# Fourier mixing and a gated feed-forward network: batch 0's row E in column tiles, by way of DRAM, with another order of the first stage

## The chip, the cores and the metric

The kernel runs on one core of a Trainium2 chip. The engines of a core are TensorE (PE: matmuls into PSUM; PEld is its weight load), VectorE (DVE), ScalarE (ACT), GpSimd (POOL) and SyncE (SP, which only issues transfers here; ScalarE and GpSimd issue some as well). Each engine carries out its own queue in order and waits on semaphores. The metric is the device time of one execution in microseconds; the kernel before takes 1946.41 us, the median of three runs (1944.94 to 1950.29).

## The reference

```python
def _attn_ref(x):                      # x: (8, 3008, 256)
    X = np.fft.fft(x, axis=1)
    X = np.fft.fft(X, axis=2)
    return X.real.astype(np.float32)

def _moe_ref(x, w_gate, w_val, w_out): # x: that result as (24064, 256); d_ff = 1536
    gate = 1.0 / (1.0 + np.exp(-(x @ w_gate)))
    val = x @ w_val
    return (gate * val @ w_out).astype(np.float32)
```

The weights come as float64 and are turned into float32 on the chip.

## The kernel before, in words

**The algebra.** The transform along the 256 features is multiplied into the weights: `merge` (L316) multiplies a piece of a weight by the table `dt` and puts the halves into `G1` (cosine rows 0 to 127) and `G2` (row 0 is the cosine row 128, the rest are sine rows). What is left for each batch is the transform along the 3008 tokens: `pk` (128 folded features with cosines), `qk` (127 with sines) and one more row, E (feature 128, with cosines). By symmetry only 1505 tokens are computed; token S-k follows from the same two sums with one sign turned.

**Sequence stage.** A batch is folded fourfold (`fold_ops`) and split into two blocks, for even and odd frequencies. The six slices `q` of a block are multiplied by a table (`ST`, cosines and sines, 377 or 376 columns) and summed into two PSUM banks `ev` and `od` (`half`); `places` adds and subtracts these into `pk` and `qk`. For batch 0 this stands in front of everything. Its E row is a third cosine group (`what` = 2): the E column is broadcast to 128 columns of the stationary matrix, so that all 128 partitions get the same row (`ek`, the third tile of `PQE[0]`). It is stored to the DRAM row `ed[0]` for later chunks. Batches 1 to 7 get their E rows together (`e_sums`): the stationary matrix has 7 columns, four column tiles of 32 hold the two blocks and the two parities of `q`, and the rows go to DRAM and come back as a broadcast (`e_rows`, tile `ek`).

**Gate groups.** A batch has six chunks of 252 (the last 246) tokens, a chunk has twelve groups `i`, one for each 128 of the 1536 hidden features. A group: `seed` takes a PSUM bank `pf` and ScalarE writes E times `ge` (row 0 of `G2`, turned onto the partitions by small transfers in `merge`) into its two halves; `front_a` adds the `pk` products; `part` copies the value (`ae`) for the mirrored tokens; `front_b` adds the `qk` products; `gate_a` and `gate_b`, one turn later, do sigmoid and product for both token halves on ScalarE and VectorE; `back` multiplies by the output weights into the banks `po`. In the very first chunk (groups 0 to 11) `seed` writes nothing. Groups 0 to 4 (`N1` = 5) add E with a matmul of `G2` by `e0`, a tile that is zero but for row 0; groups 5 to 11 have E in row 0 of `qk` and take it out again on VectorE (L614, L632).

**Weights.** A weight piece `j` (`jobs[j]`: gate, value or output, and which 256 columns or rows) is loaded by SyncE (`weight_load`), taken apart by two passes on ScalarE (`weight_parts`), joined by three operations on VectorE and an addition on GpSimd (`weight_join`), and then merged (`weight_use`: four matmuls, two ScalarE copies into `G2` and `G1`, two small `ge` transfers). Pieces 0 to 9 are loaded at the start, the others from when batch 0's input is no longer needed.

**Order.** The order on each engine is that of the program text. First come the loads, pieces 0 and 1, the folds and sequence sums with `weight_round` between the evacuations, and merge 2; then the loop over `i`. In turn `i`: `front_a(i)`, `gate_a(i-1)`, `part(i)`, `seed(i+1)`, `gate_b(i-1)`, then what `pre` and `use` hold (joins, parts and merges of later pieces), `back`, `front_b(i)`, and what `side` holds. PSUM has eight banks: five for products (`po0` to `po4`), three that `pf`, merges and sums take by turns.

## Time and profile before

| | |
|---|---|
| median of 3 runs | 1946.41 us (1944.94 to 1950.29) |
| profiled execution | 1944.18 us, span 1942.4 us |
| TensorE clock, mean granted | 0.996 |
| TensorE busy | 1913.1 us, 98% |
| first sequence matmul of batch 0 | 21.72 us |
| first gate group | 48.3 us |
| 36 sequence matmuls of batch 0 | 21.72 to 46.6 us |

Busy time is the union of an engine's instructions. A matmul in float32 appears as two passes, so that x4 are two matmuls; the ends of matmuls are modelled. A row of the timeline has the start in us, the duration in us, engine, line, operation, tiles written and read, shapes, the number of instructions merged into the row and, in brackets, the idle time before it with what ended it. SPq and ACTq are transfers that an engine issues. The chain is followed back from the last instruction to whatever released each step. In the table of waits a row says who waited for whom, with the sum in us, the number of times and the longest.

### The profile page before, as it was taken

The numbers are of one execution on the slowest core, as the hardware profiler recorded it, in microseconds if no ns is written. First come the engines' busy times: TensorE is split into PE (matmuls) and PEld (weight loads), VectorE is DVE, ScalarE is ACT, GpSimd is POOL, SyncE is SP. The second block draws the span as 40 slices with busy tenths as digits, with TensorE's granted clock in tenths as the row PEclk, the third lists the DMA queues.
The fourth block names the chain that finished last, engine by engine and source line by source line (L and its number), as shares of the span: only waits on it lengthen the run. The fifth ranks groups of instructions, "written<-read, shape, count | busy, mean of one in ns | idle before, by whom it ended". The sixth has DMA issues, their size and how long they took to land.

```text
span 1942.4 us, 34340 instructions
## 1 busy us (share of the span) xinstructions
PE 1913.1 (98%) x11180; PEld 1778.8 (92%) x11180; DVE 1445.2 (74%) x3250; ACT 1332.0 (69%) x3120; POOL 1565.7 (81%) x2802
## 2 busy tenths in 40 slices
PE   6999999999999999999999999999999999999997
PEld 4789989999999999999999999999999999999997
DVE  7667887787777877777777776777777777777776
ACT  3577657766777677776777767777677766777775
POOL 4269989997889788987889879888788986777776
PEclk9999999999999999999999999999999999999999
DMA  8343422212022111212112121111200100011011
GB/s 273 106 127 37 109 72 54 55 20 79 15 53 54 54 39 20 76 25 79 20 41 60 16 83 23 47 46 25 82 14 14 25 17 14 14 25 17 14 20 27
DMA packets 171978, 96.78 MB, mean 50 GB/s; under 512 B 136090, under 2 KB 163868, under 8 KB 169252
## 3 DMA queue, kind: packets, MB, share of 16 engines
q1 hardware_dynamic: 169842, 94.06, 20.3%
q8 instruction: 90, 1.47, 0.3%
q10 hardware_dynamic: 1926, 0.52, 0.1%
q14 instruction: 88, 0.72, 0.1%
q0 software_dynamic: 32, 0.00, 0.0%
HBM read 69.83 MB, written 46.71 MB: 60 GB/s over the span
## 4 chain that ended last, share of the span: by engine, by line
PE 96%; DVE 3%; DMA 1%; ACT 1%; issue 0%; SPq 0%; DVEq 0%
PE pf L134 49%; PE po L134 41%; PE ev L134 3%; PE od L134 1%; DVE c L719 1%; PE ps L134 1%; DMA x<-in_xf_dram 1%; DVE z L635 0%; ACT pf L648 0%; DVE h L649 0%; DVE h L647 0%; DVE os L729 0%; PE pe L134 0%; DVE x L428 0%; DVE x L392 0%
## 5 line engine op out<-in xcount | busy, mean ns | idle before, releaser
L655 POOL TENSOR_TENSOR sf<-h 128x168 f32<-128x168 f32 (+1 forms) x940 | 521.4, 574 | 225.6 <-DVE h L649 225.6
L655 POOL TENSOR_TENSOR sf<-h,sf 128x168 f32<-128x168 f32 (+1 forms) x1128 | 629.2, 578 | 59.1 <-DVE h L649 58.7
L134 PE MATMUL pf<-qk,G 128*128 128x252 f32 (+1 forms) x2304 | 582.7, 376 | 2.0 <-ACT ae L611 2.0
L134 PE MATMUL pf<-pk,G 128*128 128x252 f32 (+1 forms) x2304 | 582.8, 376 | 0.0
L649 DVE TENSOR_TENSOR h<-pf,z 128x252 f32<-128x252 f32 (+1 forms) x576 | 241.6, 419 | 427.7 <-ACT pf L648 427.7
L595 ACT ACTIVATE pf<-ek,ge 128x252 f32<-128x252 f32 (+1 forms) x1128 | 531.6, 471 | 18.5
L134 PE MATMUL po<-sf,wf 128*128 128x168 f32 (+1 forms) x3008 | 518.7, 305 | 0.0
L611 ACT ACTIVATE ae<-pf 128x504 f32<-128x504 f32 (+1 forms) x569 | 335.5, 590 | 234.9 <-PE pf L134 234.0
L134 PEld LDWEIGHTS pf<-pk,G 128*128 128x128 f32 x2304 | 436.4, 190 | 52.8 <-issue 1.6
L134 PEld LDWEIGHTS po<-sf,wf 128*128 128x128 f32 x3008 | 462.7, 190 | 8.1
L134 PE MATMUL po<-h,wf 128*128 128x168 f32 (+2 forms) x2640 | 469.2, 306 | 0.0
L719 DVE TENSOR_TENSOR c<-c 128x168 f32<-128x168 f32 (+1 forms) x929 | 438.5, 504 | 5.4 <-ACT c L696 0.2
L134 PEld LDWEIGHTS pf<-qk,G 128*128 128x128 f32 x2304 | 410.3, 190 | 34.8 <-ACT ae L611 3.3
L134 PEld LDWEIGHTS po<-h,wf 128*128 128x128 f32 x2640 | 420.1, 190 | 17.2 <-issue 0.9
L635 DVE TENSOR_TENSOR z<-ae,pf 128x504 f32<-128x504 f32 (+1 forms) x569 | 378.6, 665 | 25.2 <-ACT h L630 23.4
L630 ACT ACTIVATE h<-pf 128x252 f32<-128x252 f32 (+1 forms) x576 | 218.0, 379 | 161.3 <-PE pf L134 156.7
L648 ACT ACTIVATE pf<-z 128x252 f32<-128x252 f32 (+1 forms) x576 | 214.4, 372 | 105.7 <-DVE h L647 103.2
L647 DVE TENSOR_TENSOR h<-h,pf 128x252 f32<-128x252 f32 (+1 forms) x576 | 232.5, 404 | 0.0
L655 POOL TENSOR_TENSOR sf<-sf 128x168 f32<-128x168 f32 (+1 forms) x188 | 108.5, 577 | 14.7
L655 POOL TENSOR_TENSOR sf<-sf,h 128x168 f32<-128x168 f32 (+1 forms) x188 | 102.9, 547 | 0.0
L696 ACT COPY c<-po 128x504 f32<-128x504 f32 (+1 forms) x141 | 80.2, 569 | 2.6 <-PE po L134 2.6
L134 PE MATMUL ev<-st,x 63*128 63x189 f32 (+3 forms) x372 | 72.4, 345 | 7.7 <-DVE x L398 7.7
(141 smaller groups left out, 891.8 us busy)
## 6 DMA issues: line engine op xcount, KB each, us to landing
x<-xr SPq DMA_DIRECT2D x14, 1536.0 KB
out_dram<-os SPq DMA_DIRECT2D x372, 56.0 KB
xr<-in_xf_dram SPq DMA_DIRECT2D x14, 768.0 KB
xr<-in_xf_dram SPq DMA_DIRECT2D x35, 256.0 KB
ek<-ed SPq DMA_DIRECT2D x39, 126.0 KB
out_dram<-os SPq DMA_DIRECT2D x284, 7.0 KB
st<-in_stab_dram SPq DMA_DIRECT2D x4, 1111.9 KB
x<-in_xf_dram SPq DMA_DIRECT2D x2, 1512.0 KB
```

Of the source, the lines that this page charges most:

```text
L134: nc.tensor.matmul(o, l, r, start=start, stop=stop, skip_group_check=True)
L595: nc.scalar.activation(PF[i][:, g], EK[i // NFT], AF.Copy, scale=ge[:, g, f : f + 1])
L611: nc.scalar.activation(AP[i], PF[i], AF.Copy, scale=2.0)
L630: nc.scalar.activation(H[p][:, fh, 0:n], PF[i][:, 0], AF.Sigmoid)
L635: nc.vector.tensor_tensor(z[:, :, ::-1], AP.pop(i), PF[i], op=ALU.subtract)
L647: nc.vector.tensor_tensor(h[:, fh, 0:n], h[:, fh, 0:n], pf[:, 1], op=ALU.mult)
L648: nc.scalar.activation(pf[:, 0], z[:, 0], AF.Sigmoid)
L649: nc.vector.tensor_tensor(h[:, fh, n:], pf[:, 0], z[:, 1], op=ALU.mult)
L655: nc.gpsimd.tensor_tensor(block(p, dst), block(p, a), block(p, b), op=(ALU.subtract, ALU.add)[op])
L696: (nc.vector.tensor_copy if t == 1 or t == 3 and not last else nc.scalar.copy)(C[0][:, 3 * t * R : 3 * (t + 1) * R], PO[t][:, 0 : 3 * R])
L719: engine.tensor_tensor(t[:, dst * R : (dst + 1) * R], *v, op=(ALU.subtract, ALU.add)[op])
```

## The change

- Batch 0's E row is computed as those of the other batches: `e_sums(1)` with a stationary matrix of one column in four column tiles of bank `po4`, interleaved with the cosine groups. ScalarE copies and VectorE places it, ScalarE stores it to `ed[0:1]`, and `e_rows(0)`, issued on ScalarE as well, reads it back as a broadcast.
- `seed` writes E into PSUM for the first twelve groups too. `e0`, the extra `G2` matmuls, and the VectorE forms of `part` and `gate_a` go.
- Both sine tables are loaded ahead of piece 2.
- The second half of batch 0's fold runs wholly on VectorE; GpSimd's share of it goes.
- The order in front of the first group is new: block 0's cosines, E and block 1's by halves of `q`; then E's evacuation and store, half of the sines, piece 2 and its merge, the other sines with pieces 3 and 5 and their merges. Merges from piece 3 on go by turns into the product banks 4, 2 and 3. In the loop the pieces 6, 8, 9, ... follow with one turn between join and merge; `jobs` has its output pieces later.

```diff
     assert NPR == 6
-    jobs = [(0, 0), (1, 0), (0, 1), (1, 1), (2, 0), (0, 2), (1, 2), (2, 1), (0, 3), (1, 3), (0, 4), (2, 2),
-            (1, 4), (0, 5), (1, 5), (2, 3), (2, 4), (2, 5)]
+    jobs = [(0, 0), (1, 0), (0, 1), (1, 1), (2, 0), (0, 2), (1, 2), (2, 1), (0, 3), (1, 3), (0, 4), (1, 4),
+            (0, 5), (1, 5), (2, 2), (2, 3), (2, 4), (2, 5)]
     RAW, WS = {}, {}
     shared = {}
     KEEP = 10
...
     WO = {}
-    def weight_use(j, other=None):
+    turns = itertools.count()
+
+    def weight_use(j):
         w, c = jobs[j]
         if w == 2:
             WO[c] = WS.pop(j)
         else:
-            merge(WS.pop(j), w, c, other)
+            merge(WS.pop(j), w, c, (4, 2, 3)[next(turns) % 3] if j > 2 else None)
     def merge(ws, g, c, other):
         cs = slice(c * WC, (c + 1) * WC)
...
             ops += [lambda q=q: feat(pool, *parts[0], q) for q in qs]
         else:
-            def half1(q):
+            def half_rows(q):
                 point(nc.vector, 2, 3, q)
                 first(nc.vector, 2, 3, q)
                 for blk in range(2):
                     across(nc.vector, blk, q)
                     feat(nc.vector, *parts[blk], q)
-
-            def half2(q):
-                across(nc.vector, 0, q)
-                feat(nc.vector, *parts[0], q)
-                across(pool, 1, q)
-                feat(pool, *parts[1], q)
             for q in qs:
                 point(nc.vector, 0, 1, q)
             first(nc.vector, 0, 1, slice(0, NQ))
-            point(pool, 2, 3, qs[1])
-            first(pool, 2, 3, qs[1])
-            ops += [lambda: half1(qs[0]), lambda: half2(qs[1])]
+            ops += [lambda q=q: half_rows(q) for q in qs]
         for blk, (v, r) in enumerate(parts):
             if b and blk:
                 W[b, blk] = v[:, :, HD:D], r[:, :, HD:D]
                 continue
-            W[b, blk] = (v[:, :, 0:HD], r[:, :, 0:HD],
-                         v[:, :, HD : HD + 1].to_broadcast([v.shape[0], NQ, P]))
+            W[b, blk] = v[:, :, 0:HD], r[:, :, 0:HD], v[:, :, HD : HD + 1]
         return ops
...
     def seq_start(b):
         PQE[b] = [pqp.tile([P, NK + 1], F32, name=name, tag=name) for name in ("pk", "qk")]
-        if not b:
-            PQE[b].append(op.tile([P, NK + 1], F32, name="ek", tag="os"))
         for t in PQE[b]:
             nc.vector.memset(t[:, NK:], 0.0)
...
         tt(x8[:, :, 1], x8[:, :, 0], x8[:, :, 2], op=ALU.add)
         tt(x8[:, :, 3], x8[:, :, 0], x8[:, :, 2], op=ALU.subtract)
-    def e_sums():
+    def e_sums(m=B - 1):
         ps = bank("pe", NB - 1)
-        m = B - 1
         at_ = lambda blk, par: slice((2 * blk + par) * TB, (2 * blk + par) * TB + m)
-        for q in range(0, NQ, 2):
-            for blk in range(2):
-                c0, n = ((0, NE), (NE, NO))[blk]
-                for par in range(2):
-                    mm(ps[at_(blk, par), 0:n], x8[:, :, 1 + 2 * blk, q + par],
-                       ST[0][0:NP, 0, q + par, c0 : c0 + n], q == 0, q == NQ - 2)
-        er = op.tile([P, NK + 1], F32, name="er", tag="os")[0:m]
-        nc.vector.memset(er[:, NK:], 0.0)
-        a = evp.tile([P, 2 * NJ], F32, name="a", tag="a")[0:m, 0:NE]
-        e1 = evp.tile([P, 2 * NJ], F32, name="a", tag="a")[0:m, 0:NE]
-        nc.scalar.copy(a, ps[at_(0, 1), 0:NE])
-        nc.scalar.copy(e1[:, 0:NO], ps[at_(1, 0), 0:NO])
-
-        places(er, 0, True, a, ps[at_(0, 0), 0:NE])
-
-        def rest():
-            nc.scalar.copy(a[:, 0:NO], ps[at_(1, 1), 0:NO])
-
-        def last():
-            places(er, 1, False, e1[:, 0:NO], a[:, 0:NO])
-            nc.sync.dma_start(out=ed[1:], in_=er)
-        return rest, last
+
+        def sums(*qs):
+            for q in qs:
+                for blk in range(2):
+                    c0, n = ((0, NE), (NE, NO))[blk]
+                    w = x8[:, :, 1 + 2 * blk, q] if m > 1 else W[0, blk][2][:, q]
+                    mm(ps[at_(blk, q % 2), 0:n], w, ST[0][0:NP, 0, q, c0 : c0 + n], q < 2, q >= NQ - 2)
+
+        def even():
+            er = op.tile([P, NK + 1], F32, name="er", tag="os")[0:m]
+            nc.vector.memset(er[:, NK:], 0.0)
+            a = evp.tile([P, 2 * NJ], F32, name="a", tag="a")[0:m, 0:NE]
+            e1 = evp.tile([P, 2 * NJ], F32, name="a", tag="a")[0:m, 0:NE]
+            nc.scalar.copy(a, ps[at_(0, 1), 0:NE])
+            nc.scalar.copy(e1[:, 0:NO], ps[at_(1, 0), 0:NO])
+
+            places(er, 0, True, a, ps[at_(0, 0), 0:NE])
+
+            def rest():
+                nc.scalar.copy(a[:, 0:NO], ps[at_(1, 1), 0:NO])
+
+            def last():
+                places(er, 1, False, e1[:, 0:NO], a[:, 0:NO])
+                (nc.sync if m > 1 else nc.scalar).dma_start(out=ed[1:] if m > 1 else ed[0:1], in_=er)
+            return rest, last
+        return sums, even
+
+    def e_joint():
+        sums, even = e_sums()
+        sums(*range(NQ))
+        return even()
...
         b, c, _ = groups[i // 3]
         k0, n = chunks[c]
         EK[i // NFT] = ekp.tile([P, CH], F32, name="ek", tag="ek")[:, 0:n]
-        nc.sync.dma_start(out=EK[i // NFT], in_=ed[b : b + 1, k0 : k0 + n].to_broadcast([P, n]))
+        (nc.sync if i else nc.scalar).dma_start(out=EK[i // NFT], in_=ed[b : b + 1, k0 : k0 + n].to_broadcast([P, n]))
     PF, AP, Z = {}, {}, {}
-    N1 = 5
     def seed(i):
...
         _, _, n, f, _ = cut(i)
         PF[i] = bank("pf").rearrange("p (g n) -> p g n", g=2)[:, :, 0:n]
-        for g in range(2 if i >= NFT else 0):
+        for g in range(2):
             nc.scalar.activation(PF[i][:, g], EK[i // NFT], AF.Copy, scale=ge[:, g, f : f + 1])
     def front_a(i):
         (pk, *_), ks, _, _, fs = cut(i)
-        if i < NFT:
-            seed(i)
         for g in range(2):
-            mm(PF[i][:, g], G1[:, g, fs], pk[:, ks], i < NFT and g == 0, True)
-        for g in range(2 if i < N1 else 0):
-            mm(PF[i][:, g], G2[:, g, fs], shared["qk"][:, 4 * WC : 4 * WC + CH], False, True)
+            mm(PF[i][:, g], G1[:, g, fs], pk[:, ks], False, True)
     def part(i):
-        pqe, ks, n, f, _ = cut(i)
+        n = cut(i)[2]
         AP[i] = app.tile([P, 2, CH], F32, name="ae", tag="ae")[:, :, 0:n]
-        if not N1 <= i < NFT:
-            nc.scalar.activation(AP[i], PF[i], AF.Copy, scale=2.0)
-            return
-        for g in range(2):
-            nc.vector.scalar_tensor_tensor(out=AP[i][:, g], in0=pqe[2][:, ks],
-                                           scalar=ge[:, g, f : f + 1], in1=PF[i][:, g],
-                                           op0=ALU.mult, op1=ALU.add)
+        nc.scalar.activation(AP[i], PF[i], AF.Copy, scale=2.0)
     def front_b(i):
         (_, qk, *_), ks, _, _, fs = cut(i)
...
         if fh == 0:
             H[p] = hp.tile([P, 3, 2 * WC], F32, name="h", tag="h")[:, :, 0 : 2 * n]
         nc.scalar.activation(H[p][:, fh, 0:n], PF[i][:, 0], AF.Sigmoid)
-        if N1 <= i < NFT:
-            nc.vector.scalar_tensor_tensor(out=z[:, :, ::-1], in0=AP.pop(i), scalar=2.0, in1=PF[i],
-                                           op0=ALU.mult, op1=ALU.subtract)
-        else:
-            nc.vector.tensor_tensor(z[:, :, ::-1], AP.pop(i), PF[i], op=ALU.subtract)
+        nc.vector.tensor_tensor(z[:, :, ::-1], AP.pop(i), PF[i], op=ALU.subtract)
     def block(p, i):
...
     for j in range(2):
         weight_load(j)
     load_x(0)
-    for _ in load_table(0, NQ // 2):
-        pass
-    for j in range(2, 5):
+    for t in range(2):
+        for _ in load_table(t, NQ // 2):
+            pass
+    for j in range(2, KEEP):
         weight_load(j)
-    sines = load_table(1, NQ // 2)
-    next(sines)
-    for j in range(5, 7):
-        weight_load(j)
-    next(sines)
-    for j in range(7, KEEP):
-        weight_load(j)
-
-    def weight_round(*js):
-        for j in js:
-            weight_parts(j)
-            weight_join(j)
     weight_parts(0)
     weight_parts(1)
...
     weight_use(1)
     seq_start(0)
-    e0 = shared["qk"][:, 4 * WC : 4 * WC + CH]
-    nc.gpsimd.memset(e0, 0.0)
-    other = {(0, 0): (4, None), (0, 1): (4, None), (0, 2): (0, 1), (1, 2): (2, 3)}
-    cos = [seq_group(0, blk, what, other.get((blk, what))) for blk in range(2) for what in (0, 2)]
-    for i, f in enumerate(fold_ops(0, NQ // 2)):
+    qs = tuple(range(NQ // 2)), tuple(range(NQ // 2, NQ))
+    cos = [seq_group(0, blk, 0, (2 * blk, 2 * blk + 1)) for blk in range(2)]
+    e_, e_even = e_sums(1)
+    for f, q in zip(fold_ops(0, NQ // 2), qs):
         f()
-        for sums, _, _ in cos:
-            sums(*range(i * NQ // 2, (i + 1) * NQ // 2))
-    sin = [seq_group(0, blk, 1, other.get((blk, 1))) for blk in range(2)]
-    for i in range(2):
-        for sums, _, _ in sin:
-            sums(*range(i * NQ // 2, (i + 1) * NQ // 2))
-    evacuate = [then for _, then, _ in cos + sin]
-    for then, js in zip(evacuate, ((2, 3), (4,), (5,), (6,), (7,), (8,))):
-        weight_round(*js)
-        then()()
-    nc.scalar.dma_start(out=ed[0:1], in_=PQE[0][2][0:1])
-    nc.vector.tensor_copy(e0[0:1], PQE[0][2][0:1, 0:CH])
-    weight_parts(9)
+        cos[0][0](*q)
+        e_(*q)
+        cos[1][0](*q)
+    cos[0][1]()()
+    sin = [seq_group(0, blk, 1, (2 * blk, 2 * blk + 1)) for blk in range(2)]
+    sin[0][0](*qs[0])
+    cos[1][1]()()
+    rest, last_ = e_even()
+    rest()
+    last_()
+    sin[1][0](*qs[0])
+    weight_parts(2)
+    weight_join(2)
+    weight_use(2)
+    sin[0][0](*qs[1])
+    weight_parts(3)
+    weight_join(3)
+    sin[0][1]()()
+    e_rows(0)
+    sin[1][0](*qs[1])
+    weight_use(3)
+    weight_parts(5)
+    weight_join(5)
+    sin[1][1]()()
+    weight_use(5)
     for j in range(KEEP, KEEP + 3):
         weight_load(j)
-    weight_use(2)
     per = NFT * len(chunks)
     side = {}
...
     pre, use = {}, {}
-    for j, i in enumerate((0, 1, 2, 3, 4, 5, 6, 7, 9), 9):
+    for j, i in ((6, 0), (8, 1), (9, 2), (10, 3), (11, 4), (4, 4), (12, 5), (13, 6), (7, 6), (14, 7), (15, 8),
+                 (16, 9), (17, 10)):
         if i:
             pre.setdefault(i - 1, []).append(lambda j=j: weight_parts(j))
+        else:
+            weight_parts(j)
         pre.setdefault(i, []).insert(0, lambda j=j: weight_join(j))
         if KEEP <= j < len(jobs) - 3:
             at(i, lambda j=j: weight_load(j + 3))
-    for j, i in enumerate((0, 0, 1, 2, 0, 3, 4, 5, 4, 6, 7, 8, 8, 8, 11), 3):
+    for j, i in ((6, 1), (8, 2), (9, 3), (4, 4), (10, 4), (11, 5), (12, 6), (7, 6), (13, 7), (14, 8), (15, 9),
+                 (16, 10), (17, 11)):
         use.setdefault(i, []).append(lambda j=j: weight_use(j))
     for g in range(NG):
         for k in range(3):
             at(NFT - 2 + 3 * g + k, lambda g=g, k=k: forms(g)[k]())
-    at(N1 - 1, lambda: nc.vector.tensor_copy(PQE[0][1][0:1, 0:CH], PQE[0][2][0:1, 0:CH]))
     i0 = NFT
...
             for i, f in zip(calm(s0 if b else 3 * i0), mirror_x(b + 2)):
                 at(i, f)
+    seed(0)
     for i in range(count):
         front_a(i)
-        if N1 <= i < NFT:
-            part(i)
         if i:
             gate_a(i - 1)
-        if not N1 <= i < NFT:
-            part(i)
-        if i0 <= i + 1 < count:
+        part(i)
+        if i + 1 < count:
             seed(i + 1)
         if i:
             gate_b(i - 1)
```

More of the change, by code (lines that the diff above doesn't have):

```diff
@@ L1 @@
+import itertools
 from contextlib import ExitStack
@@ L261, in home @@
                 if j > 2:
-                    ws = some(5, pqp, "qk")[:, (j // 5) * 2 * WC : (j // 5 + 1) * 2 * WC]
+                    ws = some(4, pqp, "qk")[:, (j // 5) * 2 * WC : (j // 5 + 1) * 2 * WC]
                     return sp.tile([P, 4 * WC], F32, name="raw", tag="sf"), ws
@@ L859 @@
     later_e = []
-    at(3 * i0 + 4, lambda: later_e.extend(e_sums()))
+    at(3 * i0 + 4, lambda: later_e.extend(e_joint()))
     at(3 * i0 + 5, lambda: later_e[0]())
```

## The prediction

> **What bounds the kernel now.** I read the page first: whether one engine is full. Its busy line and its chain say that TensorE is.
>
> ```profile
> PE 1913.1 (98%) x11180; PEld 1778.8 (92%) x11180; DVE 1445.2 (74%) x3250; ACT 1332.0 (69%) x3120; POOL 1565.7 (81%) x2802
> PE 96%; DVE 3%; DMA 1%; ACT 1%; issue 0%; SPq 0%; DVEq 0%
> ```
>
> The chain in order of time, for the first 140 us, shows where the missing 2% lies. TensorE waits for loading and folding until 21.72; after that one matmul follows the other, through the sequence sums (to 46.6), the first gate group (its matmul begins at 48.3) and on to the end. So whatever the change does to TensorE's work or waits after 21.7 goes into the time one for one.
>
> ```profile
> 16.85 0.95 DVE x L388
> 17.81 1.69 DVE x L392
> ...
> 21.67 0.04 issue
> 21.72 2.88 PE ev L134 x4
> ...
> 46.75 1.73 PE ps L134 x8
> 48.48 0.85 PE pf L134 x4
> ```
>
> The timeline gives the prices of what will stand in that stretch: the first weight piece (Abs at 4.73 to its merge at 8.51), the copies behind a merge, the sigmoid, `ae` copy and seeds of a group, and the column tiles of row E (24 passes, used here for batches 1 to 7).
>
> ```profile
> 4.73 0.66 ACT L298 ACTIVATE raw<-raw 128x512 f32<-128x512 f32 x1 [2.50 <-DMA raw<-in_moe_w_gate_dram]
> 6.34 0.69 DVE L311 SCALAR_TENSOR_TENSOR raw<-raw 128x512 int32<-128x512 int32 x1
> 7.18 1.28 POOL L313 TENSOR_TENSOR raw<-raw 128x512 int32<-128x512 int32 x1 [5.08 <-DVE raw L311]
> 8.51 5.49 PE L134 MATMUL ps<-raw,dt 128*128 128x256 f32 x16 [8.51 <-POOL raw L313]
> 48.52 0.37 ACT L331 COPY G<-ps 128x256 f32<-128x256 f32 x1 [1.12 <-PE ps L134]
> 48.79 0.38 ACT L332 COPY G<-ps 128x256 f32<-128x256 f32 x1
> 118.48 0.36 ACT L630 ACTIVATE h<-pf 128x252 f32<-128x252 f32 x1
> 118.89 0.59 ACT L611 ACTIVATE ae<-pf 128x504 f32<-128x504 f32 x1
> 119.38 0.97 ACT L595 ACTIVATE pf<-ek,ge 128x252 f32<-128x252 f32 x2
> 193.14 2.09 PE L134 MATMUL pe<-st,x 126*7 126x377 f32 x24
> ```
>
> Last the windows of 2 us (core row: stretch, length and PE busy, then the other engines, granted clock, DMA share) and SyncE's waits. TensorE idles from 14.0; the clock is still full up to 18, falls within 18 to 20, and comes back near 25.8.
>
> ```profile
> 18.00:20.00 2.00, 0.00 (x0) 0.00 (x0) 1.97 (x2) 0.00 (x0) 1.63 (x2) 0.74 1.04 316
> 22.00:24.00 2.00, 2.00 (x4) 1.13 (x5) 1.92 (x5) 0.00 (x0) 0.00 (x0) 0.50 1.03 248
> 24.00:26.00 2.00, 2.00 (x4) 1.02 (x4) 1.94 (x4) 0.00 (x0) 1.34 (x1) 0.56 0.95 304
> ```
> ```profile
> SPq L291 <- DMA st<-in_stab_dram: 3.2, 1, 3.2
> ```
>
> **Start: -0.6.** All folds go to VectorE. The 126x3 addition that took 1.77 us beside GpSimd's fold (17.72; a twin of 126x6 at 13.59 took 0.17) is short now, so the first block is folded near 20.1. The first cosine table holds the start at 20.49, where SyncE's wait of 3.2 us for it ended. TensorE starts 1.2 us earlier, but at half clock until 25.8, if the clock comes back when it did: half is lost. Bounds -1.2 and 0.
>
> **TensorE's work: -9.8.** A sequence matmul of 377 columns costs 0.634 us warm (22.8 us for 36). Gone: row E's twelve, -7.6; ten `G2` x `e0` matmuls of the first five groups (0.85 us a group), -4.25. New: twelve column-tile matmuls, by the row at 193.14 2.0 us (next work 195.16). The ten merges after the first two stay ten; three of them, not one, now precede the first group.
>
> **Waits in front of the first group: +13.4.** Each engine runs its queue in order. In the new order TensorE does all cosines and E, the first halves of the sines, merge 2, the second halves, merge 3, merge 5, group 0. ScalarE does: cosine copies, three E copies, E's store to DRAM, *then* piece 2; merge 2's copies, piece 3, a sine copy, E's load from DRAM; merge 3's copies, *then* piece 5; merge 5's copies, *then* piece 6, *then* two seeds. A piece costs 3.78 us from Abs to merge (8.51-4.73: ScalarE 0.66, VectorE 0.43, 0.43, 0.69, GpSimd 1.28), and little covers it (all times of the new order are estimates, worked out from the rows):
>
> - Before merge 2, +4.6. TensorE is there at 20.5 + 7.6 + 2.0 + 3.8 + 2.65 (half clock to 25.8) = 36.5. The last cosine ended 3.8 earlier, 32.7; then two VectorE additions (0.46, 0.54), ScalarE's copy of E (0.47, waiting for their buffer), two additions of E (1.0), a copy (0.47), two additions (1.0), the store's issue (0.5, as at 45.60): 37.3. Piece 2: 41.1.
> - Before merge 3, +0.7. Merge 2 ends 42.8; TensorE has 3.8 of sines, to 46.6. Copies (0.65) and piece 3 (3.78): 47.3.
> - Before merge 5, +4.4. Merge 3 ends 49.0 with nothing behind it; 0.65 + 3.78: 53.4.
> - Before group 0, +2.9. Merge 5 ends 55.1; copies 0.65, piece 6's two ScalarE passes 1.2, two seeds 0.95: 58.0.
> - Before group 0's second half, +0.8: the `ae` copy (0.59 and the pipeline's end); piece 6's merge comes later.
>
> So group 0 begins near 58.0 instead of 48.3, with 7.7 us less left to do.
>
> **Waits in groups 1 to 8: +8.0.** The seeds (0.95 a group) move from matmuls to ScalarE. A piece's join on VectorE stands behind the last gate operation of the group before. From a group's sigmoid on: `ae` copy starts at 0.41, seeds at 0.90, second sigmoid ends 2.23, VectorE's gate product and three joins 4.2, GpSimd 5.65; only then the merge of the next turn. TensorE has 4.28 to do meanwhile (three times 0.85, a merge 1.73). Each late merge waits 1.35; it delays the next sigmoid too, so some turns come on time. Walking the turns I find merges late in turns 2, 4, 5 and 7 (2.1, 1.6, 2.9, 1.6: pieces 4 and 7, which have no merge, add 1.15 of ScalarE to two of them). From turn 8 on all is as before. In the kernel before, TensorE had 5.13 per turn and ScalarE no seeds, so this was covered. Bounds: 0, if the waits hide behind each other, and 1.35 in all seven turns plus 2.3: 11.8.
>
> **Clock: +1.7.** Two of the waits exceed 4 us. Before, 5 us of idling (14.0 to 19) dropped the clock, and it then cost half of 4.1. A wait of 4.4 to 4.6 may or may not; a cold merge costs 1.73 more. Bounds 0 and 3.4; I take one of the two.
>
> The Trainium skill, "TensorE: Matmul & The Clock Gate" (What's actually happening), says that one idle window of some 3.4 us is enough, the window running freely. An estimate from that page: a wait of 4.6 holds a whole window 0.35 of the time, one of 4.4 0.29; the term would be 1.1 on average instead of 1.7. It also means that the placing differs from run to run; no run here shows that yet.
>
> **What is hidden.** The reordered loads: the sine tables (3.65 us each, by 16.84 to 20.49) come ahead of piece 2, which moves from 26.1 to about 33.4; ScalarE reaches it at 37.3, behind its semaphore wait. Cover 3.9 us; gone, it costs what exceeds it. Second sine table: near 32, used at 42.8. E's trip: store issued at 37.3, load issued at 45.5, first used at 57.0. If each took 9 us, as the small `ge` transfers did under load (issued 12.7, SyncE passed their lanes at 21.75), it is there at 54.5. SyncE's own queue now issues pieces 10 to 12 behind merge 5's `ge` pair, near 56 instead of 47; piece 10 is used near 68. Product banks 4, 2 and 3 are free when a merge comes (E copied by 36, block 1's sines before merge 5's weights are ready); a merge costs the same in them. In groups 5 to 11 the `ae` value moves from VectorE (two of 0.43) to ScalarE (0.59): turns of 5.1 us with products cover it. The fold's added VectorE work ends near 27.4, before TensorE needs block 1's second half (30). The changed order of the later E sums is the same 24 passes.
>
> **Sum.** -0.6 - 9.8 + 13.4 + 8.0 + 1.7 = +12.7. The profiled execution took 1944.18 us (span 1942.4), 2.2 below the median 1946.41; it becomes 1956.9, and the median 1959.1.
>
> **Rivals.**
> - *Lean turns, full clock.* The turns' merges are hardly late (0 to 2) and the clock stays: -0.6 - 9.8 + 13.4 + 1 = +4.0, 1950.4. For it: ScalarE is only busy 3.9 of each turn. Against: join behind gate, in order.
> - *Transfers late.* Piece 2, or the E row, is not there. Under load `ge` needed up to 11.7 us (13.3 to 25.05): store 49.0, load 60.7, against 57.0: +3.7, together 1962.8. The start of the windows shows the transfers at their limit (share 1.03, 1.04); against it: the store is one row.
> - *Faster.* One mechanism: ScalarE's preparation of pieces 3, 5 and 6 does not bind, because their passes slip in ahead of the merge copies. Then the waits before merges 3 and 5 and 1.2 before group 0 go (-6.3), the lag that the turns inherit too (-8), the clock term shrinks (-1): -2.6, 1943.8. It decides once all waits together are below 10.4. Against: a queue keeps its order, and each copy waits for the merge that stands before the next piece.
>
> **How the numbers follow.** Likeliest (0.75): 1959, with its terms' bounds 1953 to 1964. Lean turns 0.10, transfers late 0.12, faster 0.03. The range 1952 to 1965 leaves out part of the lean and the faster case. A change of 0.3% is 5.8 us, about what a measurement of this kernel can tell from none: slower by more than that needs +5.8, which the likeliest and the late case give nearly always and the lean one hardly: 0.89; within 0.08; faster 0.03.
>
> **What would show it.** In the profile after: sequence matmuls from about 20.6; idle TensorE before `ps<-raw` (4.6, released by GpSimd), before `ps<-wqk` (0.7 and 4.4) and before `pf<-pk` (2.9, ScalarE); group 0 near 58 to 60; late merges in the first eight turns; from group 9 on nothing but a shift. Wrong if group 0 begins before 52, if the waits are put down to `ek` or weight transfers, or if the later groups differ.

## The result, and the profile after

The changed kernel takes 1965.67 us (median of 4 runs, 1964.45 to 1966.38); the kernel before, run beside it on the same chip, 1945.79. The ratio is 1.0097, with a 95% interval of 1.0079 to 1.0114: slower by about 19 us by the ratio and 19.9 by the medians, where 12.7 had been forecast. The profiled execution took 1965.09 us, its span is 1963.3 us (before 1942.4).

The page's busy line and the head of its chain of work, as shown of before:

```profile
PE 1916.0 (98%) x11160; PEld 1776.4 (90%) x11160; DVE 1439.6 (73%) x3240; ACT 1344.9 (69%) x3152; POOL 1556.0 (79%) x2795
PE 93%; DVE 3%; ACT 1%; issue 0%; DVEq 0%; ACTq 0%
```

TensorE has 20 matmul records fewer and yet is busy 2.9 us longer. The columns that explain it are in the timeline and in the windows. First the timeline of TensorE (start and length in us, engine, line, operation, operands; in brackets the idle time ahead and what ended it). These are all its waits from the first sequence matmul to group 12.

```profile
19.28 2.85 PE L135 MATMUL ev<-st,x 126*128 126x377 f32 x4 [4.18 <-DMA st<-in_stab_dram]
...
41.45 3.58 PE L135 MATMUL ps<-raw,dt 128*128 128x256 f32 x8 [4.83 <-POOL raw L314]
...
49.41 1.99 PE L135 MATMUL ps<-wqk,dt 128*128 128x256 f32 x8 [0.48 <-POOL wqk L314]
...
55.77 3.46 PE L135 MATMUL ps<-wqk,dt 128*128 128x256 f32 x8 [4.37 <-POOL wqk L314]
...
61.94 1.86 PE L135 MATMUL pf<-pk,G 128*128 128x252 f32 x4 [2.72 <-ACT pf L594]
...
64.48 2.05 PE L135 MATMUL pf<-qk,G 128*128 128x252 f32 x4 [0.68 <-ACT ae L605]
...
73.46 1.99 PE L135 MATMUL ps<-wc,dt 128*128 128x256 f32 x8 [1.37 <-POOL wc L314]
77.34 1.99 PE L135 MATMUL ps<-wf,dt 128*128 128x256 f32 x8 [0.18 <-POOL wf L314]
82.49 1.99 PE L135 MATMUL ps<-wx,dt 128*128 128x256 f32 x8 [1.46 <-POOL wx L314]
89.56 3.62 PE L135 MATMUL ps<-wx,dt 128*128 128x256 f32 x8 [3.38 <-POOL wx L314]
104.26 1.99 PE L135 MATMUL ps<-wx,dt 128*128 128x256 f32 x8 [2.56 <-POOL wx L314]
```

The five waits from merge 2 to group 0's second half add up to 13.1 us (4.83, 0.48, 4.37, 2.72, 0.68), five late merges in the turns to 8.95. Group 0 begins at 61.94 instead of 48.3, and group 12 at 122.2 instead of 100.9: 21.3 us later, with nothing after it but a shift.

Three of the rows carry a second message in their own length: a merge takes 1.99 us (49.41), but 3.58, 3.46 and 3.62 behind the long waits. The windows show why (stretch, its length, the busy time of PE, PEld, DVE, ACT and POOL, then the granted clock, the DMA share and GB/s):

```profile
38.28:41.69 3.41, 0.23 (x1) 0.24 (x2) 1.55 (x3) 0.63 (x2) 1.28 (x1) 1.00 0.93 343
41.69:45.11 3.42, 3.42 (x9) 2.71 (x9) 0.00 (x0) 0.04 (x1) 0.00 (x0) 0.50 0.05 18
51.93:55.35 3.42, 0.00 (x0) 0.00 (x0) 2.46 (x5) 1.63 (x4) 0.92 (x1) 1.00 0.04 3
55.35:58.76 3.41, 2.99 (x7) 2.46 (x8) 0.00 (x0) 0.00 (x0) 0.36 (x1) 0.50 0.00 0
58.76:62.17 3.41, 0.69 (x3) 0.29 (x3) 1.55 (x3) 2.60 (x6) 0.00 (x0) 1.00 0.08 4
62.17:65.59 3.42, 2.74 (x7) 1.70 (x7) 0.00 (x0) 1.72 (x4) 1.28 (x1) 0.50 0.88 317
65.59:69.00 3.41, 3.41 (x10) 2.73 (x9) 1.00 (x2) 1.98 (x5) 0.00 (x0) 0.50 0.37 139
86.07:89.48 3.41, 0.12 (x1) 0.00 (x0) 2.96 (x4) 1.81 (x5) 2.32 (x2) 1.00 0.05 3
89.48:92.89 3.41, 3.33 (x8) 2.70 (x9) 1.88 (x4) 2.26 (x5) 1.30 (x2) 0.50 0.60 186
99.72:103.13 3.41, 1.97 (x9) 1.33 (x7) 3.34 (x5) 2.09 (x6) 1.56 (x2) 1.00 0.04 0
103.13:106.55 3.42, 2.29 (x10) 1.85 (x11) 2.50 (x6) 1.89 (x5) 1.34 (x2) 1.00 0.35 86
```

Four stretches at half clock (cold, in what follows) come behind four of the waits, also behind the one of 2.72 us. The one behind that wait lasts for two windows, since 2.74 us of work in 3.42 did not end it. The wait of 2.56 us, which lies across 103.13, cost no clock. Half of the work done in the four stretches, 1.7, 1.5, 3.1 and 1.7 us, is 8 us in which nothing is gained. In the kernel before there was one such stretch, at the start.

What was held to be hidden was hidden. Row E's store and load in ScalarE's timeline, with the start of piece 2 and group 0's seeds, and GpSimd's last step of the pieces 3 and 5:

```profile
37.14 0.50 ACTq L556 DMA_DIRECT2D ed<-er  x1
37.68 0.66 ACT L299 ACTIVATE raw<-raw 128x512 f32<-128x512 f32 x1 [1.61 <-DVE er L501]
...
45.94 0.36 ACTq L583 DMA_DIRECT2D ek<-ed  x1
...
60.90 0.99 ACT L594 ACTIVATE pf<-ek,ge 128x252 f32<-128x252 f32 x2
...
48.06 1.29 POOL L314 TENSOR_TENSOR wqk<-wqk,raw 128x512 int32<-128x512 int32 x1 [6.66 <-DMA ek<-ed]
54.43 1.28 POOL L314 TENSOR_TENSOR wqk<-wqk,raw 128x512 int32<-128x512 int32 x1 [5.08 <-DVE wqk L312]
```

Piece 2 is begun at 37.68, when ScalarE has issued the store; the piece itself had been there since 31.5, when its last packets ended. The seeds at 60.90 begin right behind piece 6's passes, with no wait ahead; the row's last packet had ended at 48.54. One row names row E's load as what GpSimd waited for, at piece 3 (48.06). That is the profile's inference: GpSimd began before that last packet, and 0.14 us behind VectorE's end (47.92), the same distance as at piece 5 (54.29 and 54.43).

### The profile page after: what moved, and what is told of

Same layout as the page of the kernel before. It is cut to its first block, busy times and chain, and to the rows that moved or that the text cites. A ratio compares the mean times of both kernels' runs of the same rounds, so it can differ in the third digit from the quotient of the medians.

```text
span 1963.3 us, 34306 instructions
## 1 busy us (share of the span) xinstructions
PE 1916.0 (98%) x11160; PEld 1776.4 (90%) x11160; DVE 1439.6 (73%) x3240; ACT 1344.9 (69%) x3152; POOL 1556.0 (79%) x2795
## 4 chain that ended last, share of the span: by engine, by line
PE 93%; DVE 3%; ACT 1%; issue 0%; DVEq 0%; ACTq 0%
PE pf L135 48%; PE po L135 41%; PE ev L135 2%; DVE c L704 1%; PE ps L135 1%; PE od L135 1%; DVE z L620 0%; ACT pf L633 0%; DVE h L634 0%; ACT pf L594 0%; DVE h L632 0%; DVE wx L310 0%; ACT ae L605 0%; DVE os L714 0%; PE pe L135 0%
## 5 line engine op out<-in xcount | busy, mean ns | idle before, releaser
L594 ACT ACTIVATE pf<-ek,ge 128x252 f32<-128x252 f32 (+1 forms) x1152 | 542.8, 471 | 18.8
L620 DVE TENSOR_TENSOR z<-ae,pf 128x504 f32<-128x504 f32 (+1 forms) x576 | 383.3, 666 | 38.2 <-ACT h L619 36.6
L714 DVE STREAM_TRANSPOSE os<-c 128x256 f32<-128x256 f32 x192 | 73.7, 421 | 0.7 <-issue 0.6
```

Of the source, the lines that this page charges most:

```text
L594: nc.scalar.activation(PF[i][:, g], EK[i // NFT], AF.Copy, scale=ge[:, g, f : f + 1])
L620: nc.vector.tensor_tensor(z[:, :, ::-1], AP.pop(i), PF[i], op=ALU.subtract)
L714: nc.vector.transpose(os_[0][:, s, 0:nb, h, :], t[:, c0 : c0 + nb * TB])
```

## The experiments

In all of them the distance to the kernel before is taken to the runs of before on the same chip. After stands 19.9 us above its own.

Two theories were set against each other throughout. **Queues and clock**: pieces 2, 3, 5, 6 and those of the turns are prepared late because the instructions that prepare them stand behind others in the queues of ScalarE and VectorE, and each long wait that follows also costs clock. **Transfers**: the waits are for row E's way through DRAM, or for piece 2 behind the sine tables. Two more questions were whether the clock is a cost of its own, and whether ScalarE's seeds are the limit.

**Waits filled, clock kept.** Idle matmuls into a bank that nobody reads, in the four waits in front of a cold stretch.

```diff
+    FILL = {2: 10, 11: 6}
+    def filler(ps, n):
+        for _ in range(n):
+            mm(ps[:, 0:WC], dt[:, 0, 0:P], dt[:, 0, :], True, True)
...
         ps = bank("ps", other)
+        filler(ps, fill)
...
+    filler(bank("fl"), 9)
     weight_parts(5)
...
     weight_use(5)
+    filler(bank("fl", 4), 5)
```

> The kernel after with its waits left as they are, but TensorE kept busy in the four that a cold stretch followed: idle matmuls of 128x256 (0.43 us each by the merge's row) into a bank that nobody reads, ten before merge 2, nine before merge 5, five before group 0, six before the merge of piece 11. They fit into the waits of 4.83, 4.37, 2.72 and 3.38 us, so no work that counts is later. Queues and clock (mine): the four cold stretches (41.69, 55.35, 62.17 and 89.48 us) go, and with them half of the work done in them: 6 to 8 us faster than after, 1958 to 1960. Waits alone (the clock is a by-product that costs nothing, as my forecast of 1.7 nearly had it): 1964 to 1967.

Measured: 1961.64 us, ratio 1.0083 (1.0068 to 1.0098), 16.4 above before: 3.4 us gained, half of what was expected, and by the intervals not quite sure. The profile told why: the clock stayed full through the whole front, and fell instead behind merges in the turns, at 69.46, 79.70 and 100.18, where it had not fallen in after. The windows lay differently, and two waits of 1.9 us were now enough. So these were filled too.

```diff
-    FILL = {2: 10, 11: 6}
+    FILL = {2: 10, 8: 3, 10: 4, 11: 7, 13: 5}
```

> The kernel with the filled waits before group 0 once more, with idle matmuls also before the late merges of the turns (three for piece 8, four for 10, seven for 11, five for 13), behind three of which the clock had still fallen (at 69.46, 79.70 and 100.18 us, after waits of 1.9, 1.9 and 2.6). Queues and clock: those three cold stretches of 3.41 us go as well, some 4 us more, 1957 to 1959, and the clock stays full from 25 us on. Waits alone: as the kernel with the first fillings, 1961 to 1963.

Measured: 1956.84 us, ratio 1.0057 (1.0045 to 1.0070), 11.3 above before: 8.6 us gained over after, and the clock is full from 24.84 to the end. Its timeline has fillings in the place of the waits, and behind each the real work begins when it is ready: merge 2 at 41.74 (41.45 in after), merge 5 at 54.46 instead of 55.77, since the merge of piece 2 ahead of it is no longer cold:

```profile
36.73 4.48 PE L135 MATMUL ps<-dt 128*128 128x256 f32 x20
41.74 1.99 PE L135 MATMUL ps<-raw,dt 128*128 128x256 f32 x8 [0.53 <-POOL raw L314]
...
49.93 4.05 PE L135 MATMUL fl<-dt 128*128 128x256 f32 x18
54.46 1.99 PE L135 MATMUL ps<-wqk,dt 128*128 128x256 f32 x8 [0.49 <-POOL wqk L314]
```

The merges behind them take 1.99 us instead of 3.58 and 3.46. No useful work was added, and its order on every engine is the same, so the clock is a cost of its own and worth 8.6 of the 19.9 us. "Waits alone" falls.

**The order in front of group 0.** The same work, each piece prepared ahead of the copies of the merge before it.

```diff
     cos[1][1]()()
+    weight_parts(2)
+    weight_join(2)
     rest, last_ = e_even()
     rest()
     last_()
     sin[1][0](*qs[0])
-    weight_parts(2)
-    weight_join(2)
+    weight_parts(3)
+    weight_join(3)
     weight_use(2)
...
```

> The kernel after with the same work in another order on ScalarE, VectorE and GpSimd before group 0: piece 2 is prepared ahead of row E's copies, piece 3 ahead of merge 2's copies, piece 5 ahead of merge 3's, piece 6's two passes ahead of merge 5's. TensorE's order, the loads and E's way through DRAM stay. Queues: the waits in front of group 0 fall from 13.1 to about 7 (1.9 before merge 2, where piece 2's own 3.8 us from its landing near 31.5 show; 2.4 before merge 5; 1.8 and 0.8 at group 0), and cold stretches of 2 to 4 us go with them: 1955 to 1958. Transfers (the waits are for piece 2's or E's landing): no gain, 1964 to 1967.

Measured: 1956.25 us, ratio 1.0054 (1.0039 to 1.0069): 8.8 us gained, as expected of the queues.

```profile
38.12 1.99 PE L135 MATMUL ps<-raw,dt 128*128 128x256 f32 x8 [0.92 <-POOL raw L314]
47.92 2.53 PE L135 MATMUL ps<-wqk,dt 128*128 128x256 f32 x8 [2.29 <-ACT a L493]
52.07 2.05 PE L135 MATMUL pf<-pk,G 128*128 128x252 f32 x4 [1.62 <-ACT pf L594]
54.80 2.05 PE L135 MATMUL pf<-qk,G 128*128 128x252 f32 x4 [0.68 <-ACT ae L605]
```

The waits before group 0's second half are 5.5 us in sum instead of 13.1, and none is longer than 2.3. What now ends the wait before merge 5 is ScalarE's copy of the last sine block out of the product bank that this merge takes: a cover that had not mattered while the weights were later still.

**The joins a turn earlier.**

```diff
         if i:
-            pre.setdefault(i - 1, []).append(lambda j=j: weight_parts(j))
+            pre.setdefault(i - 1, []).insert(0, lambda j=j: weight_join(j))
...
-        pre.setdefault(i, []).insert(0, lambda j=j: weight_join(j))
```

The passes on ScalarE move from the turn before to two turns before, the loads with them.

> The kernel after with each piece's three passes on VectorE and one on GpSimd, and its passes on ScalarE, one turn earlier in groups 0 to 10 (the loads that wait for them as well); the first piece's join moves ahead of group 0. Queues: the late merges of the turns (1.37, 1.46, 3.38 and 2.56 us) go but for about 0.6, group 0 waits 1.2 longer, some seeds come 1 us late, and the cold stretch at 89.48 goes: 5 to 7 us faster than after, 1959 to 1961. Rival (ScalarE's seeds, not the joins, set the pace of the turns): the waits move from the merges to the gate groups' banks, and no more than 2 us are gained.

Measured: 1957.2 us, ratio 1.0059 (1.0043 to 1.0076): 7.9 us gained, a little more than expected. Of the late merges one is left, 1.39 us; group 0 waits 3.83 instead of 2.72, as the added passes stand ahead of its seeds. From group 1 on no gate group waits for its seeds (one second half waits 0.48 us for its `ae` copy), so they are not the limit. The cold stretch at 89.48 went too.

**Piece 2 ahead of the sine tables; row E's way twice as long.**

```diff
-    for t in range(2):
-        for _ in load_table(t, NQ // 2):
-            pass
-    for j in range(2, KEEP):
+    for _ in load_table(0, NQ // 2):
+        pass
+    weight_load(2)
+    for _ in load_table(1, NQ // 2):
+        pass
+    for j in range(3, KEEP):
         weight_load(j)
```

> The kernel after with piece 2 loaded ahead of the sine tables instead of behind them: it lands some 8 us earlier, each sine table 1.6 later. Queues: piece 2 is not waited for, its preparation begins behind E's copies at 36.9: 1964 to 1967, the wait before merge 2 stays at 4.8. Transfers: that wait goes, 3 to 5 us faster.

```diff
+    ed2 = dram.tile([1, NK + 1], F32, name="ed2")
...
+                if m == 1:
+                    nc.sync.dma_start(out=ed2, in_=ed[0:1])
...
-in_=ed[b : b + 1, k0 : k0 + n].to_broadcast([P, n]))
+in_=(ed[b : b + 1, k0 : k0 + n] if i else ed2[:, k0 : k0 + n]).to_broadcast([P, n]))
```

> The kernel after with row E's way through DRAM made twice as long: from the row stored, a second copy from DRAM to DRAM, and only from there the broadcast load. Queues: the row lands near 48 and is first used at 60.9, so another 3 to 6 us are hidden: 1964 to 1967. Transfers: the time grows by the added trip, 3 to 6 us: 1969 to 1972.

Measured: 1968.54 us, ratio 1.0119 (1.0104 to 1.0134), for piece 2 first; 1967.12 us, ratio 1.0114 (1.0099 to 1.0130), for the longer way. Neither gained. The four long waits stand where they stood, nearly to the hundredth; the short ones move by up to 0.7 us. First piece 2 first, then the longer way, with its longest cold stretch:

```profile
43.26 3.44 PE L135 MATMUL ps<-raw,dt 128*128 128x256 f32 x8 [4.82 <-POOL raw L314]
...
63.74 1.71 PE L135 MATMUL pf<-pk,G 128*128 128x252 f32 x4 [2.72 <-ACT pf L594]
```
```profile
23.43 2.85 PE L135 MATMUL ev<-st,x 126*128 126x377 f32 x4 [8.97 <-DMA st<-in_stab_dram]
44.55 3.78 PE L135 MATMUL ps<-raw,dt 128*128 128x256 f32 x8 [4.83 <-POOL raw L315]
...
65.83 2.05 PE L135 MATMUL pf<-pk,G 128*128 128x252 f32 x4 [2.72 <-ACT pf L597]
...
57.28:74.34 17.06, 11.61 (x26) 8.31 (x27) 4.26 (x9) 7.54 (x17) 2.56 (x2) 0.50 0.28 93
```

Piece 2's last packet ended at 25.7 us instead of 31.5, and the wait ahead of its merge is 4.82 as before: it is not a wait for that load. The longer way tests less than was meant: from the store's issue to the row's last packet it took 12.6 us instead of 11.4, as the broadcast load stands late in ScalarE's queue in both. For row E the evidence is in after itself, where the row is there 12 us ahead of its first use. So the transfer theory falls for this kernel.

Still, the first was 2.8 us further above before than after was, and the second 1.4, where no difference was expected. In both profiles the sequence sums began later than in after (20.97 and 23.43 against 19.28), behind the cosine table; in the seven other profiles with after's order of loads they began between 19.05 and 20.75. The profiled execution of the second was 4 us above its other three, and 6.0 above the one of after: its start is 4.15 later, and half of the work done cold behind the waits is 12.2 us where it is 7.9 in after. The long waits are the same; the windows lie otherwise, and the half clock from 57.28 lasted five of them. So what a wait costs in clock changes from one execution to the next (after's own four were granted 0.992, 0.992, 0.989 and 0.989 on average). Why the table lands later in some executions is not settled.

**Parts alone, in the kernel before.** First the folds on VectorE (the two fold functions made one, as in the change).

```diff
-            point(pool, 2, 3, qs[1])
-            first(pool, 2, 3, qs[1])
-            ops += [lambda: half1(qs[0]), lambda: half2(qs[1])]
+            ops += [lambda q=q: half_rows(q) for q in qs]
```

> The kernel before with one part of the change alone: all folds of batch 0 on VectorE. The first sequence matmul begins 1.2 us earlier, half of it at half clock. Mine: 0.3 to 1 us faster, 1944.9 to 1945.6 for a median of 1945.8 before; a gain of 1.2 or more if the clock comes back earlier with it.

Measured: 1945.66 us, ratio 0.9993 (0.9984 to 1.0003): no difference that can be told, and too little to tell the expected 0.3 to 1 us from nothing.

```profile
18.54 0.95 DVE L388 TENSOR_TENSOR x<-x 126x765 f32<-126x765 f32 x1 [4.06 <-DMA x<-in_xf_dram]
...
22.42 2.85 PE L134 MATMUL ev<-st,x 126*128 126x377 f32 x4 [7.15 <-DMA st<-in_stab_dram]
```

The folds did get shorter: the 126x3 addition takes 0.16 us instead of 1.77, and from the landing of the input to the first folded block it is 3.2 us (18.54 to 21.74) instead of 4.8 (16.85 to 21.67). But in this execution the input landed 1.7 us later than in the profile of before, and the cosine table later still. In the profile of before the folds ended TensorE's wait (7.72 us, VectorE's L398), here the table did: which of them holds the start changes with the landing of the loads.

Then row E in column tiles, by way of DRAM into the broadcast tile that the kernel before had filled by matmuls.

```diff
-    cos = [seq_group(0, blk, what, other.get((blk, what))) for blk in range(2) for what in (0, 2)]
+    cos = [seq_group(0, blk, 0, (2 * blk, 2 * blk + 1)) for blk in range(2)]
+    e_, e_even = e_sums(1)
...
+        rest, last = e_even()
+        rest()
+        last()
+        ek = op.tile([P, NK + 1], F32, name="ek", tag="os")
+        nc.sync.dma_start(out=ek, in_=ed[0:1].to_broadcast([P, NK + 1]))
...
-    for then, js in zip(evacuate, ((2, 3), (4,), (5,), (6,), (7,), (8,))):
+    for then, js in zip((evacuate[0], evacuate[1], None, evacuate[2], evacuate[3]), ((2,), (3,), (4,), (5, 6), (7, 8))):
```

> The kernel before with one part of the change alone: row E in column tiles, its row stored to DRAM and loaded back as a broadcast tile; loads, preparation of the pieces, the first five groups' matmuls with E and the merges as before. TensorE has 5.6 us less to do ahead of group 0 (twelve matmuls of 0.634 for twelve column-tile ones of 2.0 together). If that work sets the end: 1940 to 1941. If the sine tables do, which land near 33.7 and 40.2 in the order of before and are then wanted near 31 and 37.8: waits of 3 and 2.5 us take the place of the work, 1945 to 1947.

Measured: 1950.93 us, ratio 1.0029 (1.0017 to 1.0040), slower by 5 us, outside both expectations.

```profile
35.56 1.50 PE L134 MATMUL ev<-st,x 126*128 126x377 f32 x4 [0.91 <-DMA st<-in_stab_dram]
42.37 1.55 PE L134 MATMUL ev<-st,x 126*128 126x377 f32 x2 [2.78 <-DMA st<-in_stab_dram]
53.83 1.12 PE L134 MATMUL pf<-wqk,G 128*128 128x252 f32 x4 [3.12 <-DVE wqk L839]
```

The two waits for the sine table were expected. The third was not: I had put the preparation of pieces 7 and 8 ahead of the last sine block's additions in VectorE's queue, and the copy of row E behind them. It is the change's own fault once more, made in another place. With those two pieces behind:

```diff
-((2,), (3,), (4,), (5, 6), (7, 8))
+((2,), (3,), (4,), (5,), (6,))
...
+    weight_round(7, 8)
     weight_parts(9)
```

> The kernel with row E's part alone once more, with pieces 7 and 8 prepared behind the last sine block and row E's copy instead of ahead of them, so that the wait of 3.12 us at group 0 (VectorE's queue, of my own making) goes. What stays are the waits for the two halves of the sine table (0.9 and 2.8 measured) and the cold stretch behind the second: 5.6 us less work against 3.7 of waits and 1.7 of clock: 1945 to 1947. If row E's way through DRAM is what group 0 waits for: 1949 to 1951 again, with the wait put down to the row's load.

Measured: 1945.97 us, ratio 1.0002 (0.9993 to 1.0011): the same as before. 5.6 us less work (twelve matmuls of 0.634 for 2.0) came to nothing: TensorE waited 1.86 us for the second half of the sine table and 1.89 at group 0, where VectorE's copy of row E stood behind its other work and then 0.35 us for the row's load; of the rest, some 0.9 is clock (half until 27.49 instead of 25.77) and 0.7 the column tiles, which take 1.36 us for six of the twelve at full clock (31.91 to 33.27), not 1.0. As these two runs read, row E's cheaper sums pay only if the sine tables come earlier, which the change does, and if the pieces are ready earlier, which it does not; no run adds these to the kernel before one by one.

**All of it, prepared ahead.** The changed kernel with both orders above, piece 2's load ahead of the sine tables, the sine copies ahead of merge 3, and group 0's seeds ahead of merge 5.

```diff
     sin[0][1]()()
     e_rows(0)
     sin[1][0](*qs[1])
-    weight_use(3)
-    weight_parts(5)
-    weight_join(5)
     sin[1][1]()()
+    weight_use(3)
+    seed(0)
     weight_use(5)
+    weight_join(6)
+    weight_parts(8)
...
```

> The kernel after, with its row E in column tiles by way of DRAM, its folds on VectorE, its seeds and its product banks, but everything prepared ahead: pieces 2, 3, 5 and 6 before the copies of the merges that run before them, the sine blocks copied before merge 3, group 0's seeds before merge 5, joins one turn ahead of their merges, and piece 2's load ahead of the sine tables. Queues and clock: of the 13.1 us of waits before group 0 some 2 stay, of the 9 in the turns 1.5, and the cold stretches go: 22 to 25 us faster than after and 3 to 7 faster than before: 1939 to 1943. If ScalarE's seeds were the limit, or E's way through DRAM too long: 1946 to 1955.

Measured: 1940.39 us (10 runs), ratio 0.9975 (0.9966 to 0.9985): faster than both kernels, 24.7 us less against before than after has, as expected.

```profile
38.31 1.99 PE L135 MATMUL ps<-raw,dt 128*128 128x256 f32 x8 [0.30 <-POOL raw L314]
46.93 1.97 PE L135 MATMUL ps<-wqk,dt 128*128 128x256 f32 x8 [1.10 <-ACT a L493]
49.49 1.12 PE L135 MATMUL pf<-pk,G 128*128 128x252 f32 x4 [0.59 <-ACT pf L594]
51.66 1.12 PE L135 MATMUL pf<-qk,G 128*128 128x252 f32 x4 [1.05 <-ACT ae L605]
62.82 1.12 PE L135 MATMUL pf<-qk,G 128*128 128x252 f32 x4 [0.58 <-ACT ae L605]
69.81 1.99 PE L135 MATMUL ps<-wx,dt 128*128 128x256 f32 x8 [1.38 <-POOL wx L314]
```

The waits sum to 5.0 us instead of 22, none is long enough to cost clock, and the seeds, the product banks and the column tiles are the change's own. Now the seeds wait 1.11 us for row E's load: with everything else early, its way through DRAM has come up to the edge.

**How long a wait costs clock.** Waits put in on purpose where TensorE is else never idle, of two kinds.

```diff
+        for _ in range(k):
+            ts(out=qk[:, 0:CH], in0=qk[:, 0:CH], scalar1=1.0, scalar2=None, op0=ALU.mult)
+        ts(out=pk[:, 0:CH], in0=pk[:, 0:CH], scalar1=1.0, scalar2=None, op0=ALU.mult)
+        ts(out=pk[:, CH:], in0=pk[:, CH:], scalar1=1.0, scalar2=None, op0=ALU.mult)
```

> The kernel after with waits put in on purpose every seventh turn from group 96 on, where TensorE is else never idle: 2, 4, 6, 8, 11, 14 or 17 passes of VectorE (times 1.0, in place) over the first columns of the sine rows, then two over the cosine rows, all of which the next group's first matmul waits for. The result of the passes is the same row. What is read is, for each length of wait, how often the granted clock falls behind it and for how long. A single idle window of about 3.4 us needed whole: no drop for waits under 3.4, and for longer ones a share (wait - 3.4) / 3.4. A window that need only be mostly idle, as the waits of 2.7 to 4.8 us of the kernel after hint: drops from waits of about 2.5 on, and for nearly all above 4. Each drop costs 1.7 us or a multiple of it.

```diff
+        for _ in range(k):
+            nc.vector.tensor_scalar(out=pk[:, 0:64], in0=pk[:, 0:64], scalar1=1.0, scalar2=None, op0=ALU.mult)
+        nc.vector.tensor_scalar(out=pk[:, CH : CH + 8], in0=pk[:, CH : CH + 8], scalar1=1.0, scalar2=None, op0=ALU.mult)
```

> As the kernel with waits put in every seventh turn, but shorter ones: 4 to 24 narrow passes of VectorE over the first 64 columns of the cosine rows and one over 8 columns, early in the turn, for which the next group's first matmul waits. The result of the passes is the same row. Waits of 0.3 to 4 us are to come of it. If one mostly idle window is enough, the clock falls behind some of the waits between 1.5 and 3.4 us and behind none under 1; if the window must be all idle, behind none under 3.4.

Their times, 2508 and 2301 us, say nothing but that VectorE was held up as well; the first kind gave no wait under 3.3 us. Together they hold waits of 0.4 to 9.6 us, most with no second one near them. Of these, none of the eight under 2.2 us cost clock, eight of the eleven between 2.4 and 3.4 us did, and all the longer ones. Two of the second kind, one with and one without:

```profile
494.02:497.43 3.41, 0.97 (x7) 0.71 (x5) 2.89 (x11) 1.21 (x4) 0.23 (x1) 1.00 0.00 0
497.43:500.85 3.42, 3.42 (x8) 2.84 (x9) 2.97 (x8) 1.56 (x4) 2.45 (x5) 0.50 0.00 0
1272.26:1275.67 3.41, 1.65 (x12) 1.37 (x10) 3.05 (x13) 0.09 (x1) 0.00 (x0) 1.00 0.03 6
1275.67:1279.08 3.41, 1.79 (x8) 1.53 (x9) 2.07 (x5) 3.38 (x9) 2.58 (x7) 1.00 0.48 72
```

A wait of 2.45 us lay in one window, which was busy for 0.97 us, and the clock fell at its end. A wait of 3.38 us was cut in two by the edge at 1275.67, both windows were about half busy, and it did not fall. The expectation's first branch, a window that is idle as a whole, is refuted.

## Why the prediction was right or wrong

The direction, the mechanism and the places were right: after is slower, outside the measurement's doubt, from work late in the queues of ScalarE and VectorE. The size was not: 12.7 forecast, 19.9 measured, and the time 0.7 us above the range. Group 0 began at 61.94, not at 58 to 60: the cold stretches stand ahead of it.

- **Clock, +1.7: the step that failed.** It was priced as one of two waits over 4 us costing one cold merge. It is 8.6 us by the kernel with all waits filled (7.9 by the windows). Two things were missed: waits of 2.7 and 3.4 us cost clock as well, and one stretch lasted two windows, because group 0, with a further wait inside, was not busy enough to end it. With 8.6 in place of 1.7 the forecast sum becomes +19.6, against 19.9 measured. That it comes so close is partly luck: the other terms' misses, below, add some 2.5 us, and the two profiled executions are 20.9 apart.
- **Waits in front of group 0, +13.4: right.** 4.83, 0.48, 4.37, 2.72 and 0.68 against 4.6, 0.7, 4.4, 2.9 and 0.8; the kernel with the order turned round confirms the cause.
- **Late merges, +8.0: right in size** (8.95), with 1.37, 0.18, 1.46, 3.38 and 2.56 in turns 2, 3, 4, 5 and 7, where 2.1, 0, 1.6, 2.9 and 1.6 had been put. Earlier joins take all but 1.39 us of it away.
- **Start, -0.6: too small, and half of it luck.** The first sequence matmul came 2.44 us earlier, at 19.28, of which some 1.8 is kept (cold work went from 4.05 to 5.35 us, and half of the 1.3 is lost). The folds were shortened as forecast, but that alone would have led to the table's landing, put at 20.49; in this execution the table landed 1.2 us earlier than that, which the change does not explain, and in one other execution with the same loads TensorE waited for it until 23.43.
- **TensorE's work, -9.8: nearly right.** The column tiles take 1.36 us for six (29.30 to 30.66), 2.7 for the twelve and not 2.0, which leaves -9.2. The row that the 2.0 was taken from had all 24 passes in one piece.
- **A term that was left out, +2.5.** A wait costs TensorE some 0.25 us more than its idle time. A group's matmuls take 1.01 us up to the end of the last, while the next can start 0.85 us behind them (94.71 and 95.56), and a merge behind a wait takes 1.83 us to the next row (73.46 to 75.29) instead of 1.73. There are ten waits. To group 12, 21.3 us later in the profile, the terms then make -1.8 + 22.0 + 7.9 - 9.2 + 2.5 = +21.4.
- **What was held to be hidden** was hidden: piece 2's later load, row E's way through DRAM (12 us ahead of its use), the pieces 10 to 12, the product banks. So the rival *transfers late* is out, though its 1962.8 was nearer to the time; had it come in, the number would have been near and the cause wrong. *Lean turns, full clock* failed at both of its conditions. *Faster* named the right lever: once the preparation slips in ahead of the copies the waits are 5.0, under its mark of 10.4, and that kernel took 1940.39 where it gave 1943.8.

The prediction weighed a rule of the Trainium skill, "TensorE: Matmul & The Clock Gate" (What's actually happening): the clock falls behind an idle window of some 3.4 us, in a grid that runs freely. The window's length and the free grid are as the traces show them (3.413 us; counted from the first sequence matmul an edge lies at 22.4 us in after and at 20.2 in the kernel with the longer way, so the work does not set the grid; waits of 2.56 and 3.38 us across an edge did no harm). That the window must be idle is not: 20% busy (58.76) and 28% busy (494.02) were little enough. The estimate drawn from it, 1.1 us, was further off than the 1.7 taken.

## What to carry to other kernels

Freeing an engine that is the bound pays only as far as the work that feeds it is ready by then: read, for each piece, where its preparation stands in every queue, and move it ahead of the copies that wait for the engine. When TensorE gets a new wait, price its clock with it: in these runs about 2 us of waiting within one window of 3.4 us halved the clock of the next, and further waits there kept it low. Filling the waits with idle matmuls won back 8.6 us here; taking most of the waits away, and the cold stretches with them, won 24.7.

## What the runs showed of the hardware

From the clock records and the matmul records of the two kernels with waits put in I worked out, for each window of 3.413 us between 0 and 1900 us, the share that matmuls cover and the clock of the window behind it.

| clock of the window | busy share | windows | next one at full clock |
|---|---|---|---|
| full | up to 0.40 | 95 | 0 |
| full | 0.43 and more | 845 | 845 |
| half | up to 0.80 | 66 | 0 |
| half | 0.82 | 2 | 1 |
| half | 0.83 and more | 94 | 94 |

I had expected neither the sharpness nor the distance between the two marks. The clock falls when a window is less than some 0.42 busy, and comes back only after one that is busy for more than 0.82. In the other kernels of this study the marks hold too, but for a few windows within 0.04 of the lower one (one at 0.41 kept the clock, two at 0.44 lost it), about the doubt in the modelled ends of the matmuls. It explains both surprises of the result: the wait of 2.72 us that lay in one window, and the window from 62.17, busy for 0.80, that did not bring the clock back.
